# Second attention scores: each head alone on 64 rows of the array instead of both heads on 128 rows

## The chip, the core and the metric

The kernel runs on one core of a Trainium2 chip. A core has a matrix engine (TensorE; PE for its matmuls and PEld for its weight loads in the profile), VectorE (DVE), ScalarE (ACT), GpSimd (POOL) and a queue engine (SP) that issues most DMAs. Matmuls write to PSUM, which has eight banks of 128 partitions by 512 fp32 values; VectorE and ScalarE read the banks out. The metric is device time in microseconds of the one core, and less is better.

## The reference

Two attentions follow each other, and then two mixer layers. With 8 batches, 8 heads, 576 positions, head size 64 and 32 packing vectors per head:

```python
def sm_attn(qq, kk, vv):
    s = scale * np.matmul(qq, kk.transpose(0, 1, 3, 2))
    s = s - np.max(s, axis=-1, keepdims=True)
    a = np.exp(s)
    a = a / (np.sum(a, axis=-1, keepdims=True) + 1e-09)
    return np.matmul(a, vv)
p_packed = sm_attn(p, k, v)                # 32 rows per head over 576 keys
out = sm_attn(q, p_packed, p_packed)       # 576 rows per head over those 32
...
x = mixer_1(x)   # r * v: sigmoid(xr @ w_r) * (relu(xk @ w_k)**2 @ w_v), xk and xr mixed with the row before
x = mixer_2(x)   # u + relu(u @ w_ch1) @ w_ch2, with u = x + its low-rank mix over positions
```

The scores of the second attention, `qq @ kk.T` with 576 queries, 32 keys and 64 terms per head, are what the change is about. They are computed in plain fp32.

## The kernel before, in words

**Units.** A unit of attention is two batches (`b2`) by two heads (`h`). There are 16 units. The generator `attention_steps` writes one: it transposes keys, packing vectors and queries on the matrix engine, makes the first scores in `sps` (two banks), their softmax, the packed rows `pp` (128 x 128: 64 rows a batch, 32 a head; a mask `hmask` zeroes, in each row, the 64 columns of the other head), their transpose `ppt`, and then the second scores. `qt` holds the transposed queries: rows 0 to 63 are head 0, rows 64 to 127 head 1. The softmax of the second scores is `a2` (20 groups of 32 keys, in the order column block, batch, head), which is transposed into `th` and multiplied with `ppz` to give `xo`.

**The stretch of the change.** Line 197 records every matmul, line 209 every transpose. Before, eight matmuls multiply a 128 x 128 block of `qt` with 64 columns of `ppt` (both heads of a batch) into the bank `psa`, and one more with 128 columns into `psb`. The zeroes in `ppt` keep the heads apart. Then VectorE takes, bank by bank, the maximum of each group of 32 (line 274, `s2`) and subtracts it (line 251, into `a2`). In fp32 a matmul is two records of PE and two of PEld in the trace, so the nine are 18.

**Stages.** The first eight units run at the start, four at a time in lanes of their own buffers, advanced by turns: each `yield` of the generator ends a turn. In this stage inputs and weights are loaded and cast, and the first mixer's `psr` matmuls come in between. The other eight units run in the middle of the first mixer's matmuls (`psk`, `psv`, `psr`, `psu`), with two banks for themselves (`ps_a`). After them comes the second mixer (`psc`).

**What sets the order.** Everything is recorded in a plan first. `emit` then walks through a model of the engines: each operation has a cost, an engine takes the ready operation of the lowest class and, on the matrix engine and the SP queue, the lowest sequence number, and a bank is granted to the request that can have it earliest. The engines then execute the written order. So a change of an operation's cost or of the number of turns moves other work as well, most of all in the first stage.

Of the kernel before, what the change touches and what calls it, by code (L numbers as in the profile page):

```python
# [14 lines left out]
ALU = mybir.AluOpType  # L15
# [459 lines left out]
def packed_attention_moe_mixer_kernel(  # L475
# [19 lines left out]
    NP = p.shape[2]  # L495
    P = 128
# [20 lines left out]
    plan = Plan(nc)  # L517
    add, sub, mul = ALU.add, ALU.subtract, ALU.mult
# [35 lines left out]
    def ps_att():  # L554
        return plan.bank(att_banks[0], "psat", att_banks[0] is ps_a)
# [89 lines left out]
    def attention_steps(A, u, u_next):  # L645
# [7 lines left out]
        qt, at = A.big(F32, "qt"), A.big(F32, "at")  # L653
# [37 lines left out]
        for b2 in range(2):  # L691
            for h in range(2):
                o = slice(b2 * 64 + h * 32, b2 * 64 + (h + 1) * 32)
                for r in range(2):
# [3 lines left out]
                            start=True, stop=True, skip_group_check=True)  # L698
        for b2 in range(2):
            for h in range(2):  # L700
                o = slice(b2 * 64 + h * 32, b2 * 64 + (h + 1) * 32)
# [12 lines left out]
        for b2 in range(2):  # L714
            r = slice(b2 * 64, (b2 + 1) * 64)
# [32 lines left out]
        for t in range(5):  # L748
            for g in range(4):
                o = t * P + g * 32  # L750
# [3 lines left out]
                        start=(t == 0), stop=(t == 4), skip_group_check=True)  # L754
# [11 lines left out]
        ppt = plan.tile(A.one, [P, P], F32, "ppt")  # L766
        plan.copy(ppt, ps[:, 0:P])

        yield
        psa = ps_att()  # L770
        for ip in range(4):
            for b2 in range(2):
                plan.mm(psa[:, ip * P + b2 * 64:ip * P + (b2 + 1) * 64],
                        qt[:, b2 * 512 + ip * P:b2 * 512 + (ip + 1) * P],
                        ppt[:, b2 * 64:(b2 + 1) * 64], start=True, stop=True)
        yield
        psb = ps_att()
        plan.mm(psb[:, 0:P], qt[:, 1024:1152], ppt, start=True, stop=True)
        if A.first:
            a2 = A.big(F32, "a2", (0, 1))[:, 0:20 * NP].rearrange("p (g k) -> p g k", k=NP)  # L780
        else:
            a2 = plan.tile(A.one, [P, 20, NP], F32, "a2", parts=(0, 1))
        s2 = plan.tile(A.one, [P, 4, 20], F32, "s2", parts=(0, 1))
        for g, src, g0, g1 in ((0, psa, 0, 16), (1, psb[:, 0:P], 16, 20)):
            sv = src.rearrange("p (g k) -> p g k", k=NP)
            plan.reduce(s2.at(g)[:, 0, g0:g1], sv, ALU.max)
            plan.tt(a2.on(g)[:, g0:g1, :], sv,
                    s2.at(g)[:, 0, g0:g1].unsqueeze(2).to_broadcast([P, g1 - g0, NP]), sub)
        plan.act(a2, a2, AF.Exp, scale=SCALE)
        plan.reduce(s2[:, 1, :], a2, add)  # L790
        plan.ts(s2[:, 2, :], s2[:, 1, :], 1e-9, None, add)
# [14 lines left out]
        for b2 in range(2):  # L806
            r = slice(b2 * 64, (b2 + 1) * 64)
# [7 lines left out]
        for c0, c1 in ((256, 576), (0, 256)):  # L815
# [4 lines left out]
            for n, (lh, rh) in enumerate(terms):  # L820
                for b2 in range(2):
                    r = slice(b2 * 64, (b2 + 1) * 64)
                    plan.mm(pss[b2][:, 0:w], ppz[r, lh, :], rh[r, c0:c1], start=(n == 0),
                            stop=(n + 1 == len(terms)))
# [7 lines left out]
    def attention(A, u, u_next):  # L832
        for _ in attention_steps(A, u, u_next):
            pass
# [104 lines left out]
    plan.cls = 0  # L939
    A0.after = go  # L940
    steps = [attention_steps(lane[u], u, nxt[u]) for u in range(NLEAD)]
    prev = {w: u for u, w in nxt.items()}
    step = 0
# [47 lines left out]
    for b2 in range(2):  # L991
        r = slice(b2 * 64, (b2 + 1) * 64)
# [5 lines left out]
    for i0, i1 in ((0, NI),):  # L998
        src = uv[:, i0 * NP:i1 * NP]
# [360 lines left out]
    for n in range(2, len(chunks)):  # L1360
# [32 lines left out]
        if n >= CAST0:  # L1393
            plan.cls = 3
            for _ in range(len(casts) if n == NCAST else NPER):
                if casts:
                    rows, src, size, put = casts.pop(0)
# [119 lines left out]
```

## Time and profile before

| what | value |
|---|---|
| median of 3 runs | 1522.26 us (1520.06 to 1522.84) |
| the profiled execution | 1520.6 us, of which its span 1518.8 us |
| matrix engine, matmuls | 1486.8 us busy, 98% of the span |
| VectorE | 926.4 us busy, 61% |
| ScalarE | 692.2 us busy, 46% |
| granted clock of the matrix engine | 0.985 of full speed on average |

A busy share says how long an engine had something to do, not that it worked at its peak. A group row reads: line, engine, operation, output<-inputs, shapes, count, then busy time and mean duration in ns, then the idle time just before these instructions and what ended it. In a row of a matmul, `128*128` is the number of rows and columns of the array that it uses, and what follows is the shape that it streams.

### The profile page before, as it was taken

The page shows a single profiled execution, that of the slowest core. Times are in us where ns is not written, and L with a number is a line of the kernel's source. Part 1 is how long each engine was busy: PE and PEld are TensorE (multiplying, and loading weights), DVE is VectorE, ACT ScalarE, POOL GpSimd, SP SyncE. Part 2 cuts the span into 40 slices and gives each one's busy share as a digit, 9 for nine tenths or more (in the row PEclk, how much of TensorE's full clock was granted, in tenths as well). Part 3 has the DMA queues.
Part 4 walks back from the last instruction along what each step waited for, and adds up shares of the span by engine and source line. Part 5 has one row for each costly group of instructions (what it writes and reads, how often), then busy time and mean ns, then how long its engine had stood idle before and what let it go on. Part 6 is the DMA issues. An engine that isn't in the chain of part 4 may idle for free.

```text
span 1518.8 us, 25744 instructions
## 1 busy us (share of the span) xinstructions
PE 1486.8 (98%) x9456; PEld 1300.8 (86%) x9456; DVE 926.4 (61%) x2092; ACT 692.2 (46%) x1595; POOL 269.3 (18%) x522
## 2 busy tenths in 40 slices
PE   6899999999999999999999999999999999999998
PEld 5668888888888888889899898989999999989997
DVE  6687967778777878776645363545435454444533
ACT  5577556666676666666422232322223232322321
POOL 0000000000000000001333333333333333333331
PEclk8689999999999999999999999999999999999999
DMA  9973354664754446666969677696867768676763
GB/s 226 233 184 131 106 134 115 185 177 125 202 154 135 157 130 207 212 217 193 313 160 243 160 199 196 167 242 159 232 159 212 184 169 222 164 216 163 203 168 103
DMA packets 202188, 275.66 MB, mean 181 GB/s; under 512 B 68944, under 2 KB 95888, under 8 KB 202064
## 3 DMA queue, kind: packets, MB, share of 16 engines
q0 software_dynamic: 72576, 132.15, 33.9%
q1 hardware_dynamic: 129488, 141.87, 31.8%
q8 instruction: 76, 1.25, 0.3%
q14 instruction: 48, 0.39, 0.1%
HBM read 221.45 MB, written 52.50 MB: 180 GB/s over the span
## 4 chain that ended last, share of the span: by engine, by line
PE 92%; DMA 3%; DVE 2%; SPq 1%; ACT 1%; issue 1%; DVEq 0%
PE psc L197 49%; PE psk L197 13%; PE psv L197 13%; PE psr L197 6%; PE psat L197 5%; PE psat L209 3%; DMA qin<-in_q_dram 1%; PE psh L197 1%; PE pst L209 1%; SPq L316 1%; PE psu L197 1%; DMA kin<-in_k_dram 1%; DMA s<-w_d 1%; DMA st<-in_moe_w_r_dram 0%; DMA raw_v<-v_d 0%
## 5 line engine op out<-in xcount | busy, mean ns | idle before, releaser
L197 PE MATMUL psc<-w,hid 128*128 128x512 f32 x1728 | 446.6, 393 | 0.7 <-ACT xu L285 0.7
L197 PEld LDWEIGHTS psc<-ob,wb 128*128 128x128 f32 x3024 | 406.7, 190 | 27.1
L197 PE MATMUL psc<-ob,wb 128*128 128x256 f32 x3024 | 420.3, 283 | 0.0
L316 POOL DMA_DIRECT2D wb<-ws_d x504 | 266.2, 529 | 585.1 <-PE psc L197 491.1
L197 PEld LDWEIGHTS psc<-w,hid 128*128 128x128 f32 x1728 | 306.0, 189 | 51.6 <-ACT xu L285 1.1
L197 PE MATMUL psk<-xk,wk 128*128 128x384 f32 x1056 | 210.3, 341 | 2.0 <-DVE wk L270 1.6
L251 DVE TENSOR_TENSOR tmp<-tmp,psc 128x256 f32<-128x256 f32 x288 | 120.8, 420 | 143.5 <-PE psc L197 140.9
L197 PE MATMUL psv<-wv,kk 128*128 128x512 f32 x783 | 205.9, 398 | 0.0
L230 ACT ACTIVATE hid<-tmp 128x256 fp32r<-128x256 f32 x216 | 85.2, 417 | 262.8 <-DVE tmp L251 262.6
L197 PEld LDWEIGHTS psk<-xk,wk 128*128 128x128 f32 x1056 | 184.2, 188 | 11.1 <-DVE wk L270 2.2
L197 PEld LDWEIGHTS psv<-wv,kk 128*128 128x128 f32 x783 | 143.5, 188 | 29.1 <-issue 1.4
L270 DVE SCALAR_TENSOR_TENSOR hid<-psc,hid 128x256 fp32r<-128x256 f32 x72 | 30.5, 424 | 187.6 <-ACT hid L230 187.6
L197 PE MATMUL psr<-wr,xr 128*128 128x512 f32 x414 | 110.9, 401 | 1.4 <-ACT rs L285 0.6
L285 ACT ACTIVATE tmp<-psc 128x256 f32<-128x256 f32 x144 | 54.6, 379 | 125.2 <-PE psc L197 125.2
L270 DVE SCALAR_TENSOR_TENSOR hid<-tmp,hid 128x256 fp32r<-128x256 f32 x216 | 86.4, 423 | 23.3 <-ACT hid L230 15.0
L308 POOL MEMSET x<- 128x8 f32 x4 | 0.5, 114 | 550.6 <-DVE m L267 375.8
L197 PEld LDWEIGHTS psr<-wr,xr 128*128 128x128 f32 x414 | 75.1, 188 | 19.1 <-ACT rs L285 1.2
L230 ACT ACTIVATE sq<-psk 128x384 f32<-128x384 f32 x96 | 46.6, 490 | 68.8 <-PE psk L197 68.1
L230 ACT ACTIVATE hid<-psc 128x256 fp32r<-128x256 f32 x72 | 27.5, 382 | 102.1 <-PE psc L197 102.0
L251 DVE TENSOR_TENSOR kk<-sq,kk 128x384 fp32r<-128x384 f32 x87 | 47.9, 553 | 35.9 <-ACT kk L285 35.8
L267 DVE SCALAR_TENSOR_TENSOR m<-x,mu_t,m 128x384 f32<-128x384 f32 x88 | 52.1, 611 | 0.9 <-ACT m L230 0.7
L230 ACT ACTIVATE m<-x,om_t 128x384 f32<-128x384 f32 x88 | 50.6, 607 | 1.5 <-DVE xr L251 0.9
(174 smaller groups left out, 1704.4 us busy)
## 6 DMA issues: line engine op xcount, KB each, us to landing
wb<-ws_d POOLq DMA_DIRECT2D x504, 256.0 KB, 3.1
st<-in_moe_w_ch_dram SPq DMA_DIRECT2D x32, 512.0 KB, 5.2
ws_d<-wb SPq DMA_DIRECT2D x56, 256.0 KB, 3.0
qin<-in_q_dram SPq DMA_DIRECT2D x32, 288.0 KB, 6.4
x_d<-xo SPq DMA_DIRECT2D x16, 576.0 KB, 3.8
x_d<-x SPq DMA_DIRECT2D x36, 256.0 KB, 2.2
u<-x_d SPq DMA_DIRECT2D x36, 256.0 KB, 5.9
out_dram<-u SPq DMA_DIRECT2D x36, 256.0 KB, 3.8
```

What stands on the lines that cost most here:

```text
L197: self.nc.tensor.matmul(o, l, r, start=start, stop=stop, **k)
L209: self.nc.tensor.transpose(out.get(), in_.get(), ident.get())
L230: self.nc.scalar.activation(o, in_.get(), func, **k)
L251: return self.elem(engs, lambda e, o, x, y: e.tensor_tensor(out=o, in0=x, in1=y, op=op), out, [a, b], self.TT, cls)
L267: ("dve",), lambda e, o, x, y, z: e.scalar_tensor_tensor(out=o, in0=x, scalar=z, in1=y, op0=op0, op1=op1), out, [a, b, s], {"dve": (1.042, ...
L270: ("dve",), lambda e, o, x, y: e.scalar_tensor_tensor(out=o, in0=x, scalar=s, in1=y, op0=op0, op1=op1), out, [a, b], self.TT, cls)
L285: self.nc.scalar.activation(o, i, AF.Copy)
L308: (self.nc.gpsimd if eng == "pool" else self.nc.vector).memset(o, 0.0)
L316: (self.nc.sync if eng == "sp" else self.nc.gpsimd).dma_start(out=o, in_=i)
```

## The change

Each head gets a bank of its own, `ph[0]` and `ph[1]`. Each matmul now uses the 64 rows of one head of `qt` and the 32 keys of that head of one batch, so the nine matmuls become 20. Heads alternate in the written order. Both banks are asked for at once, and one `yield` goes. VectorE again does two maxima and two subtractions, now of 320 values each, and the subtraction writes every second group of `a2`.

```diff
         yield
-        psa = ps_att()
+        ph = [ps_att() for _ in range(2)]
         for ip in range(4):
             for b2 in range(2):
-                plan.mm(psa[:, ip * P + b2 * 64:ip * P + (b2 + 1) * 64],
-                        qt[:, b2 * 512 + ip * P:b2 * 512 + (ip + 1) * P],
-                        ppt[:, b2 * 64:(b2 + 1) * 64], start=True, stop=True)
-        yield
-        psb = ps_att()
-        plan.mm(psb[:, 0:P], qt[:, 1024:1152], ppt, start=True, stop=True)
+                for h in range(2):
+                    r = slice(h * 64, (h + 1) * 64)
+                    o = b2 * 64 + h * 32
+                    plan.mm(ph[h][:, ip * 64 + b2 * 32:ip * 64 + (b2 + 1) * 32],
+                            qt[r, b2 * 512 + ip * P:b2 * 512 + (ip + 1) * P],
+                            ppt[r, o:o + 32], start=True, stop=True, skip_group_check=True)
+        for b2 in range(2):
+            for h in range(2):
+                r = slice(h * 64, (h + 1) * 64)
+                o = b2 * 64 + h * 32
+                plan.mm(ph[h][:, 256 + b2 * 32:256 + (b2 + 1) * 32], qt[r, 1024:1152],
+                        ppt[r, o:o + 32], start=True, stop=True, skip_group_check=True)
...
-        for g, src, g0, g1 in ((0, psa, 0, 16), (1, psb[:, 0:P], 16, 20)):
-            sv = src.rearrange("p (g k) -> p g k", k=NP)
-            plan.reduce(s2.at(g)[:, 0, g0:g1], sv, ALU.max)
-            plan.tt(a2.on(g)[:, g0:g1, :], sv,
-                    s2.at(g)[:, 0, g0:g1].unsqueeze(2).to_broadcast([P, g1 - g0, NP]), sub)
+        av = a2.rearrange("p (g h) k -> p g h k", h=2)
+        for h in range(2):
+            sv = ph[h][:, 0:320].rearrange("p (g k) -> p g k", k=NP)
+            mx = s2.at(h)[:, 0, h * 10:(h + 1) * 10]
+            plan.reduce(mx, sv, ALU.max)
+            plan.tt(av.on(h)[:, :, h, :], sv, mx.unsqueeze(2).to_broadcast([P, 10, NP]), sub)
```

In the order of the matrix engine, this is the ninth unit, in the middle of the first mixer, before. A row is line, operation, output<-inputs, the partitions and columns of the output, and the count; `psv` and `psk` are the mixer's matmuls and `psat` is any bank of attention:

```order
L209 MATMUL psat<-ident,pp 128x128
L197 MATMUL psv<-wv_1894,kk 128x512 x6
L197 MATMUL psk<-xk,wk_1_1890 128x384
L197 MATMUL psat<-ppt,qt 128x64 x8
L197 MATMUL psat<-ppt,qt 128x128
L197 MATMUL psk<-xk,wk_1_1890 128x384 x2
```

And the same place of the changed kernel:

```order
L209 MATMUL psat<-ident,pp 128x128
L197 MATMUL psv<-wv_1968,kk 128x512 x6
L197 MATMUL psat<-ppt,qt 128x32 x20
L197 MATMUL psk<-xk,wk_1_1964 128x384 x3
```

The nine matmuls became 20 in one piece, between the same neighbours give or take one `psk`; all eight units of this stage look like this.

In the first stage the order moves more. The matrix engine about the seventh unit, before (`psr` belongs to the mixer, `a_178` and `a_1385` are the first and the second softmax of two units, `th,ppz` is the last product of a unit):

```order
L197 MATMUL psat<-th,ppz 128x256 x2
L197 MATMUL psr<-wr_184,xr 128x512 x2
L209 MATMUL psat<-ident,pp 128x128
L197 MATMUL psr<-wr_181,xr 128x512 x3
L197 MATMUL psr<-wr_182,xr 128x512
L197 MATMUL psat<-ppt,qt 128x64 x5
L209 MATMUL psat<-ident,a_178 128x128 x2
L209 MATMUL psat<-ident,a_1385 128x128 x4
L209 MATMUL psat<-ident,a_178 128x128 x2
L209 MATMUL psat<-ident,a_1385 128x128
L197 MATMUL psat<-ppt,qt 128x64 x3
```

And the changed kernel about the same unit:

```order
L209 MATMUL psat<-ident,pp 128x128
L197 MATMUL psr<-wr_184,xr 128x512 x4
L197 MATMUL psat<-ppt,qt 128x32 x2
L197 MATMUL psat<-th,ppz 128x320 x2
L197 MATMUL psat<-ppt,qt 128x32 x14
L197 MATMUL psat<-th,ppz 128x256
L197 MATMUL psat<-ppt,qt 128x32 x2
L197 MATMUL psat<-th,ppz 128x256
L197 MATMUL psat<-ppt,qt 128x32 x2
L197 MATMUL psr<-wr_181,xr 128x512 x3
```

The second scores of one unit are cut into four pieces there, with the last products of another unit between them (which also use 64 rows), and the transposes that stood between them before stand elsewhere.

## Rows read from the trace of the kernel before

**Rows 1.** The page: busy time, share of the span and instructions of each engine.
```profile
PE 1486.8 (98%) x9456; PEld 1300.8 (86%) x9456; DVE 926.4 (61%) x2092; ACT 692.2 (46%) x1595; POOL 269.3 (18%) x522
```
**Rows 2.** The page: the chain that ended last, shares of the span.
```profile
PE 92%; DMA 3%; DVE 2%; SPq 1%; ACT 1%; issue 1%; DVEq 0%
```
**Rows 3.** Busy time by stage: from:to and length, engines in turn, clock, DMA share, GB/s.
```profile
0.00:60.00 60.00, 43.06 (x451) 33.88 (x451) 39.28 (x109) 36.34 (x106) 1.31 (x11) 0.85 0.96 221
60.00:86.00 26.00, 21.68 (x94) 15.07 (x94) 15.05 (x35) 12.12 (x35) 0.00 (x0) 0.50 1.11 264
86.00:140.00 54.00, 51.73 (x515) 39.40 (x514) 47.14 (x117) 42.75 (x114) 0.00 (x0) 1.00 0.49 141
230.00:545.00 315.00, 314.25 (x2117) 265.05 (x2116) 243.18 (x544) 207.56 (x462) 0.12 (x1) 1.00 0.53 153
22.00:28.00 6.00, 5.76 (x26) 4.98 (x26) 4.20 (x11) 3.07 (x9) 0.00 (x0) 0.50 1.09 242
```
**Rows 4.** Waits of PE in 0 to 150 us, the longest: total, times, longest.
```profile
PE psat L209 <- DMA kin<-in_k_dram: 7.7, 3, 3.7
PE psat L209 <- DMA qin<-in_q_dram: 5.1, 4, 1.6
```
**Rows 5.** Waits of PE in 230 to 545 us, all of them.
```profile
PE psu L197 <- DVE xs L288: 0.5, 1, 0.5
PE psu L197 <- DVE xs L251: 0.2, 1, 0.2
```
**Rows 6.** Timeline of PE at a late unit: start, length, engine, what, count.
```profile
520.46 2.17 PE L197 MATMUL psat<-ppt,qt 128*128 128x64 f32 x18
522.38 0.71 PE L197 MATMUL psv<-wv,kk 128*128 128x512 f32 x2
```
**Rows 7.** The same for PEld, with the mixer's loads after it.
```profile
520.24 2.20 PEld L197 LDWEIGHTS psat<-ppt,qt 128*128 128x128 f32 x18
522.36 0.30 PEld L197 LDWEIGHTS psv<-wv,kk 128*128 128x128 f32 x2
522.70 2.17 PEld L197 LDWEIGHTS psk<-xk,wk 128*128 128x128 f32 x12
524.86 1.98 PEld L197 LDWEIGHTS psv<-wv,kk 128*128 128x128 f32 x9
```
**Rows 8.** Timeline of PE at an early unit, at half clock.
```profile
62.31 4.05 PE L197 MATMUL psat<-ppt,qt 128*128 128x64 f32 x18
66.15 0.85 PE L209 MATMUL psat<-ident,qin 128*128 128x128 f32 x3
```
**Rows 9.** Timeline of PEld at 498.2 us: loads on 64 rows.
```profile
498.21 0.18 PEld L197 LDWEIGHTS psat<-th,ppz 64*128 64x128 f32 x1 [0.37 <-PE psr L197]
498.21 0.29 PEld L197 LDWEIGHTS psat<-tl,ppz 64*128 64x128 f32 x2
498.32 0.33 PEld L197 LDWEIGHTS psat<-th,ppz 64*128 64x128 f32 x2
```
**Rows 10.** Timeline of PE from 505 to 509 us: first scores inside the mixer.
```profile
504.74 1.72 PE L197 MATMUL psk<-xk,wk 128*128 128x384 f32 x9
506.40 0.66 PE L197 MATMUL psat<-kh,pT 64*32 64x256 f32 x16
506.85 0.31 PE L197 MATMUL psat<-kt,pT 64*32 64x64 f32 x8
507.09 1.68 PE L197 MATMUL psk<-xk,wk 128*128 128x384 f32 x8
508.61 0.63 PE L197 MATMUL psu<-xs,ust 128*128 128x512 f32 x2
```
**Rows 11.** The same for PEld.
```profile
506.39 0.18 PEld L197 LDWEIGHTS psat<-kh,pT 64*32 64x32 f32 x16 [0.25 <-issue]
```
**Rows 12.** Groups of VectorE by form, whole span.
```profile
L274 DVE TENSOR_REDUCE s<-psat 128x16 f32<-128x512 f32 x16 | 11.0, 688 | 8.9 <-PE psat L197 8.9
L251 DVE TENSOR_TENSOR a<-psat,s 128x512 f32<-128x512 f32 x16 | 10.9, 683 | 0.0
L274 DVE TENSOR_REDUCE st<-psat 128x1 f32<-128x320 f32 x16 | 7.8, 487 | 7.3 <-PE psat L197 7.1
L274 DVE TENSOR_REDUCE s<-psat 128x4 f32<-128x128 f32 x16 | 4.5, 282 | 0.0
L251 DVE TENSOR_TENSOR a<-psat,s 128x128 f32<-128x128 f32 x16 | 4.5, 282 | 0.0
```

## Prediction

> **What bounds the kernel now.** I read the busy shares first: the matrix engine is busy 98% of the span, VectorE 61% [rows 1]. The chain of waits agrees, with 92% on the matrix engine [rows 2]. But a share is an average over stages, and the second scores run in two of them, so the table by stage comes next [rows 3]. In 230 to 545 us, where the last eight units lie among the mixer's matmuls, the engine is busy 314.25 of 315 us at full clock, and its waits add up to 0.7 us [rows 5]. There every microsecond of matrix work, more or less, is one of the total, and a later result of VectorE costs nothing while other matmuls are at hand. In the first stage it is otherwise. From 0 to 60 us the engine is busy 43 of 60 us and its longest waits are for inputs, 7.7 and 5.1 us [rows 3, 4]; from 60 to 86 us it has half the clock (1.2 of 2.4 GHz) and DMA queues are full; from 86 to 140 us it is busy 51.7 of 54 us at full clock.
>
> **Part 1: the loads of a burst.** Before, a unit's second scores take from 520.46 to 522.38 us, 1.92 us for 18 records, that is 0.107 us each, and the loads come at the same pace: 18 from 520.24, the next group at 522.36 [rows 6, 7]. So the weight loads (128 columns each) set the pace and the matmuls hide behind them: to stream 64 columns takes less time than to load 128. The change makes 20 matmuls, 40 records with 40 loads, of which two at a time lie on different halves of the array. What does a load on 64 rows cost? At 498.21 us two of them, one on each half, start within 0.01 us, and the next pair follows at 498.32 [rows 9]. So the halves do load side by side, and a pair needs about 0.11 us, as one load on 128 rows does: a load on half the rows is not shorter, since it still has 128 columns. Twenty pairs are 20 x 0.11 = 2.2 us. The streaming gets shorter (32 columns in place of 64), but it was hidden already.
>
> The Trainium skill weighs both ways here. "TensorEngine Tiling (Array Packing)", section "Theoretical Speedup", gives up to 2x for row tiling when the contraction is 64 or less, which would make the burst an estimated 0.96 us. Against it, "TensorE: Matmul & The Clock Gate", section "LDWEIGHTS (loading the stationary operand)", says that a load's time goes by its columns, whatever its rows, and the trace agrees with its 0.11 us for a pair on 64 rows. The tiling page's "Instruction Overhead" warns in the same sense not to take a tiling factor from a dimension that is small already.
>
> **Part 2: going into the half-array mode and back.** Before, the burst stands among matmuls on 128 x 128, without a break. After, it needs another division of the array, in which loads don't run ahead. What that costs is seen at the first scores, which are on 64 x 32 [rows 10, 11]: the load engine stands idle for 0.25 us before them. In all: nine psk matmuls from 504.74 at 0.18 us each (12 loads take 2.16 us [rows 7]) end at 506.36; after the burst, eight until 508.61 have their first slot at 508.61 - 1.44 = 507.17. Of these 0.81 us the streaming takes 0.45 (506.40 to 506.85) and about 0.11 for the short ones (two rounds of 64 columns, estimated by the 0.45 for two rounds of 256). About 0.25 to 0.3 us is left for going in and out. I take 0.3, since loads there have 32 columns and here 128.
>
> A burst then costs 2.2 + 0.3 = 2.5 us in place of 1.92: 0.58 more. Eight of them in the mixer, where nothing hides it: +4.6 us. The bounds are as follows. If a pair of loads took half of the 0.11 us, a burst would cost 1.1 + 0.3 = 1.4, that is 0.5 less; if the two halves did not load side by side, 4.4 + 0.3 = 4.7, 2.8 more.
>
> **Part 3: the first stage.** The same work comes with four units up to 86 us and four behind it. Its bursts are cut into pieces, which cost nothing as long as everything is on 128 x 128, but now each piece between other work is a way in and out. Counted in the two orders of the matrix engine, changes of the array's division grow by 17 up to the first psr and by 10 from there to the last of these units; each is half of 0.3. From 86 us on that is 10 x 0.15 + 4 x 0.28 = 2.6 us on an engine that is 96% busy, and I count all of it. Before 86 us it is 17 x 0.15 + 4 x 0.28 = 3.7 us, more for the burst at half clock (3.84 us for 18 records [rows 8], double), of which the waits for inputs hide a part: 17 of the first 60 us and 4 of the next 26 are idle. I take 2 us of it; the ends are 0 and 5.
>
> **Part 4: VectorE, banks, turns.** Removed per unit: 688 + 683 + 282 + 282 = 1935 ns. Added: two maxima and two subtractions of 320 values, 4 x 487 = 1948 ns by the 320-wide maximum [rows 12]. That is no change. The first maximum now waits for nearly the whole burst, where before it waited for the first bank, eight of nine matmuls: some 0.2 us later. In the mixer this is covered by 0.7 us of waits in 315 [rows 5]; without that cover it would be 8 x 0.2 = 1.6 us. Two banks are held in both cases. One yield less moves each later step of a unit one turn ahead; SP's loads change places by a few rows (a qin behind two reads of x), with no bytes more. I take 0 for this, with 3 us to either side, since the idle time that a better order could fill from 86 to 140 us is 54 - 51.7 = 2.3 us.
>
> **Sum.** 4.6 + 2.6 + 2 = +9.2 us. On the profiled execution of 1520.6 us that is 1529.8; the median of the runs is 1.7 us above that execution, so I forecast 1531 us, with 1525 to 1537 as this case's own range.
>
> **The rivals.**
> - *Cheap halves, faster.* A load on 64 rows with short streaming behind it goes at a quicker pace than the trace shows, and a pair costs half, 0.055 us. Then a burst takes 1.4 us, the eight in the mixer give back 4.2, the first stage nothing (its ways in and out eat it): 1518 us. It decides from the point where a pair takes under (1.92 - 0.3) / 20 = 0.08 us. For it: in the trace the 64-row loads stand before matmuls that stream 256 or 320 columns, never 32. Against it: the second pair in [rows 9] came 0.11 us after the first although nothing had to stream yet. The Trainium skill's 2x ("TensorEngine Tiling (Array Packing)", "Theoretical Speedup") would go this way. Chance 13%.
> - *The first stage hides its share.* Inputs bound it and the order fills the gaps: only 4.6 us remain, 1527 us, or 1524 with a lucky order. For it: full DMA queues up to 86 us [rows 3]. Against it: 96% busy from there on. Chance 17%.
> - *The clock falls.* In the early burst at half clock the engine did nothing but second scores for 3.84 us, and the clock stayed low [rows 3, 8]; so this work, even on all rows, did not raise it. On half the rows, the same burst at full clock may let it fall. A stay like 22 to 28 us [rows 3] costs 3 us; at half of the bursts this is 8 x 3 = 24 us more, 1555; once or twice, 1537. Against it: the first scores (64 x 32) and the last products (64 x 128) stand in the mixer at full clock from 230 to 545 us. Chance 12%.
> - *The halves don't run side by side* when the matmuls are short: +2.8 us a burst, 16 of them, 1567 us. [rows 9] speak against it. Chance 4%.
>
> **How the numbers follow.** The forecast has 54%. Within 0.2% of before, about what a measurement of this kernel can tell from no change, is 1519.2 to 1525.3: some of the second rival (its lower part) and the edge of the first and of the forecast, 14%. Faster: most of the first rival and a lucky order, 15%. Slower: 71%. For 8 times in 10 the range goes from 1518, below which most of the cheap halves lie, to 1542, above which are the many falls of the clock and the serial halves.
>
> **What would show it.** PE and PEld each have 16 x 22 = 352 records more. A late burst of 40 records lasts 2.1 to 2.3 us from its first record to its last, with pairs of loads 0.11 us apart and a gap of about 0.25 us ahead of it; 230 to 545 us gets about 4.6 us longer with waits as small as now. The clock in that stage stays at 1.00. The end of the first eight units moves by 3 to 7 us. I am wrong if pairs of loads come at 0.08 us or less, if the clock's row in the mixer is below 1.00, or if the first stage ends no later than now.

## The result and the profile after

The change made the kernel slower: 1538.08 us median (1532.12 to 1543.68, 4 runs) against 1522.55 (1520.06 to 1523.3, 4 runs), a ratio of 1.0116 with a 95% interval of 1.0093 to 1.0138. A second series on another occasion gave 1541.62 us (1539.42 to 1545.81, 4 runs), ratio 1.0141 (1.0124 to 1.0158). The sign is the one forecast. The two medians lie within 1518 to 1542 us, the range for 8 times in 10, but above 1525 to 1537, the case's own range, and the loss is 15.5 and 20.2 us by the medians where +9 was forecast. In the first series the runs also lie 3.6 times as far apart as those of before (11.6 us against 3.2).

The page of the changed kernel, its first line of busy times, beside [rows 1]:

```profile
PE 1501.8 (98%) x9808; PEld 1312.4 (86%) x9808; DVE 927.9 (61%) x2102; ACT 690.4 (45%) x1585; POOL 269.4 (18%) x522
```

The matrix engine has the 352 records more that were counted on, and 15 us more of busy time; VectorE has no more to do.

A late unit of the changed kernel on PE, to be read against [rows 6]:

```profile
529.71 1.12 PE L197 MATMUL psk<-xk,wk 128*128 128x384 f32 x5
530.76 2.42 PE L197 MATMUL psat<-ppt,qt 64*128 64x32 f32 x40
533.11 0.62 PE L197 MATMUL psk<-xk,wk 128*128 128x384 f32 x2
```

And on PEld, against [rows 7]:

```profile
530.76 2.31 PEld L197 LDWEIGHTS psat<-ppt,qt 64*128 64x128 f32 x40 [0.25 <-issue]
533.11 0.48 PEld L197 LDWEIGHTS psk<-xk,wk 128*128 128x128 f32 x3
```

From the first record to the next work it is 2.35 us in place of 1.92, and the load engine stands idle for 0.25 us before. That is the burst of the forecast: 20 pairs of loads, 0.11 us apart, and a way in and out.

The stages of the changed kernel, in the columns of [rows 3]:

```profile
0.00:60.00 60.00, 45.24 (x479) 35.51 (x479) 36.71 (x104) 34.31 (x101) 1.32 (x11) 0.83 0.97 224
60.00:86.00 26.00, 21.45 (x196) 14.22 (x194) 20.83 (x50) 16.48 (x43) 0.00 (x0) 0.80 1.05 248
86.00:140.00 54.00, 52.28 (x521) 41.44 (x521) 40.81 (x104) 33.77 (x92) 0.00 (x0) 0.84 0.49 147
230.00:545.00 315.00, 312.54 (x2285) 261.38 (x2284) 241.13 (x544) 202.11 (x450) 0.12 (x1) 1.00 0.54 154
```

The reader is to look at the clock, the third number from the right. In the mixer it is 1.00, as before. From 60 to 86 us it is higher than before (0.80 against 0.50), but from 86 to 140 us, where the engine is busy 97% of the time, it is 0.84 against 1.00: some 17 of these 54 us at 1.2 GHz. This is the fastest but one of eight runs (1533.45 us). The profile of the second series shows the slowest one (1545.81 us), in the same view:

```profile
0.00:86.00 86.00, 67.27 (x613) 51.67 (x614) 52.92 (x141) 44.97 (x123) 1.31 (x11) 0.71 0.97 226
86.00:140.00 54.00, 52.55 (x522) 40.23 (x521) 36.74 (x96) 32.36 (x95) 0.00 (x0) 0.78 0.48 132
0.00:150.00 150.00, 129.83 (x1192) 99.49 (x1193) 99.19 (x258) 85.09 (x234) 1.31 (x11) 0.75 0.75 185
```

Where a run lost its time can be told by two landmarks, the first `psu` (the mixer is well under way, the first eight units are done) and the first `psc` (the second mixer begins). The engine has the same records between them in both kernels, but for those of the change. In these rows the shortest, median and longest duration in ns come first, then the first and the last start in us. The kernel before:

```profile
L197 PE MATMUL psu<-xs,ust x72: 390/397/505, 219.0 to 735.5; 128*128 128x512 f32 x72
L197 PE MATMUL psc<-ob,wb x3024: 274/283/368, 721.0 to 1510.3; 128*128 128x256 f32 x189
```

The changed kernel, first series:

```profile
L197 PE MATMUL psu<-xs,ust x72: 390/397/504, 225.7 to 748.3; 128*128 128x512 f32 x72
L197 PE MATMUL psc<-ob,wb x3024: 274/283/365, 733.7 to 1523.2; 128*128 128x256 f32 x189
```

The changed kernel, second series:

```profile
L197 PE MATMUL psu<-xs,ust x72: 389/397/506, 235.3 to 757.9; 128*128 128x512 f32 x72
L197 PE MATMUL psc<-ob,wb x3024: 273/283/417, 743.4 to 1535.5; 128*128 128x256 f32 x189
```

Between the landmarks lie 502.0, 508.0 and 508.1 us: the mixer with the late units costs 6 us more, and it costs this in both. Up to the first landmark it is 6.7 us more in the one and 16.3 in the other. So the mixer has a fixed price near the forecast, and most of what was missed, and of what differs from run to run, is in the first stage. Another 2.6 us of the slower run lie behind the second landmark: there the matrix engine waits 2.2 us for `xu` (0.7 in the kernel before), and a stay of 3.4 us at half clock follows.

### The profile page after: what moved, and what is told of

Read it like the earlier page. It is cut to its first block, busy times and chain, and to the rows that moved or that the text cites. A ratio compares the mean times of both kernels' runs of the same rounds, so it can differ in the third digit from the quotient of the medians.

```text
span 1531.7 us, 26453 instructions
## 1 busy us (share of the span) xinstructions
PE 1501.8 (98%) x9808; PEld 1312.4 (86%) x9808; DVE 927.9 (61%) x2102; ACT 690.4 (45%) x1585; POOL 269.4 (18%) x522
## 4 chain that ended last, share of the span: by engine, by line
PE 92%; DMA 3%; DVE 2%; SPq 1%; ACT 1%; issue 1%; DVEq 0%; ACTq 0%
PE psc L197 49%; PE psk L197 13%; PE psv L197 13%; PE psr L197 7%; PE psat L197 5%; PE psat L209 3%; DMA qin<-in_q_dram 1%; PE psh L197 1%; PE pst L209 1%; PE psu L197 1%; SPq L316 1%; DMA s<-w_d 1%; DMA kin<-in_k_dram 0%; DMA vin<-in_v_dram 0%; DMA st<-in_moe_w_v_dram 0%
## 5 line engine op out<-in xcount | busy, mean ns | idle before, releaser
L197 PEld LDWEIGHTS psat<-ppt,qt 64*128 64x128 f32 x640 | 44.2, 196 | 8.1 <-issue 2.2
```

Source lines behind the costliest of these rows:

```text
L197: self.nc.tensor.matmul(o, l, r, start=start, stop=stop, **k)
```

## Experiments

Ratios are to runs of the kernel before in the same series (medians 1520.5 to 1521.4 us). "Clock" is the median over a kernel's runs of the mean granted clock; before it is 0.987 or 0.988. The first row, "streams twice", "four times, first eight units" and "heads in turn" are of one series; the two stages alone, the turns and "four times" of another; the last three rows of two more.

| kernel | median us | ratio (95%) | clock |
|---|---|---|---|
| as changed, again | 1541.62 | 1.0141 (1.0124 to 1.0158) | 0.978 |
| late eight units alone | 1527.91 | 1.0054 (1.0039 to 1.0069) | 0.986 |
| first eight units alone | 1528.36 | 1.0042 (1.0024 to 1.0060) | 0.980 |
| old matmuls, new turns and banks | 1516.40 | 0.9969 (0.9952 to 0.9986) | 0.990 |
| each new matmul streams twice | 1532.95 | 1.0086 (1.0067 to 1.0104) | 0.986 |
| four times | 1530.17 | 1.0071 (1.0059 to 1.0083) | 0.991 |
| four times, first eight units | 1530.76 | 1.0069 (1.0056 to 1.0082) | 0.991 |
| heads in turn | 1575.95 | 1.0365 (1.0334 to 1.0396) | 0.965 |
| order of before, half the streaming | 1521.04 | 1.0006 (0.9995 to 1.0017) | 0.985 |
| changed order, 128 rows | 1522.81 | 1.0013 (1.0002 to 1.0025) | 0.990 |
| changed order, 128 rows, half the streaming | 1526.73 | 1.0030 (1.0017 to 1.0043) | 0.984 |

**The change in one of the two stages.** Both sets of matmuls and of VectorE's operations stand in the code, and the unit decides:

```diff
+        new = u >= NLEAD      # the other kernel: u < NLEAD
+        if new:
             ph = [ps_att() for _ in range(2)]
             ...
+        else:
+            psa = ps_att()
             ...
```

> The change in the last eight units alone (those in the middle of the first mixer); the first eight are as before, in the same order on the matrix engine. Theory (two costs that add: a fixed one of a burst in the mixer, and one of the first stage that came out larger than forecast): each late burst costs 0.4 to 0.55 us more, 8 of them 3.5 to 4.5 us, so about 1526.5 us, with the clock at full speed through the mixer. Rival (the clock falls in the mixer, or later work there is delayed): more than 8 us, 1530 us or above. Rival (the late part is hidden and all of the loss is in the first stage): within 1 us of before.

> The change in the first eight units alone; the matrix engine's order is that of the changed kernel up to the mixer. Theory: it carries the larger part of the loss and its spread, 8 to 15 us, so 1530 to 1538 us, with runs apart by several us, the slower ones at a lower mean clock. Rival (the first stage costs what was forecast, 4.6 us, and the rest comes later): 1527 us with a spread as before, 3 us.

The late units cost 8.2 us by the ratio, the first eight 6.4, together 14.6 of the 18 to 21 by the ratios of the whole change. The late bursts last 2.35 us each and the mixer is at full clock, as the theory has it; between the landmarks there are 506.7 us, 4.7 more than before. The other 3.5 us by the ratio were not expected. The profiled run of it was its slowest (1531.67 us). In it 2.8 us more than before lie behind the second landmark, with a wait of 2.1 us for `xu` as above, and it has two stays at half clock outside the units (0.83 over 10 us, at 170 and at 745 us). How much of this the faster runs have isn't known.

The first eight alone gave runs from 1520.88 to 1532.0 us, at clocks of 0.987 and 0.975; the late eight alone lie from 1523.94 to 1531.67. So the larger part of the spread is the first eight's, but not all. The median of this kernel, 1528.36 us, is under the 1530 of my theory and close to the rival's 1527. Up to the first landmark this kernel does need 10.9 us more than before (229.9 us), as the theory has it; but between the landmarks it needs 498.4 us, 3.6 less than before, with the same matmuls there. What differs there is the written order of the mixer, which the first stage shifts: it is worth some 4 us by itself.

**The turns and banks alone.**

```diff
         yield
-        psa = ps_att()
+        psa, psb = [ps_att() for _ in range(2)]
...
-        yield
-        psb = ps_att()
         plan.mm(psb[:, 0:P], qt[:, 1024:1152], ppt, start=True, stop=True)
```

> The matmuls as before (nine on 128 rows, psa and psb), but both banks asked for at once and one yield less, as in the change. Theory (the new matmuls are the cause): within 3 us of before, 1520 to 1526 us. Rival (the order that one turn less gives is the cause in the first stage): 1528 us or more, with the first stage later by 5 us or more.

It is 0.3% faster than before, 4 us by the medians, 1 beyond my 3. The matmuls are to blame, then, not the turns. Its landmarks:

```profile
L197 PE MATMUL psu<-xs,ust x72: 387/393/501, 219.5 to 732.2; 128*128 128x512 f32 x72
L197 PE MATMUL psc<-ob,wb x3024: 274/283/365, 717.7 to 1506.6; 128*128 128x256 f32 x189
```

The gain is in the mixer (498.2 us, 3.8 less than before). The matrix engine's waits for `xs` are down to 0.2 us from 0.7 there [rows 5], which is 0.5 of it; what makes up the rest no run here shows. This is the version that beats both kernels.

**The clock, by what is streamed.** A burst's pace is set by its loads, so that each matmul can stream its 32 columns again, onto columns of the bank that a later one overwrites (`REP` is 4 or 2; the last four matmuls of a unit get the same edit, which is left out here):

```diff
-                    plan.mm(ph[h][:, ip * 64 + b2 * 32:ip * 64 + (b2 + 1) * 32],
+                    plan.mm(ph[h][:, ip * 64 + b2 * 32:ip * 64 + b2 * 32 + 32 * REP].rearrange("p (a k) -> p a k", k=NP),
                             qt[r, b2 * 512 + ip * P:b2 * 512 + (ip + 1) * P],
-                            ppt[r, o:o + 32], start=True, stop=True, skip_group_check=True)
+                            ppt[r, o:o + 32].unsqueeze(1).to_broadcast([64, REP, NP]),
+                            start=True, stop=True, rep=REP, skip_group_check=True)
...
```

> The changed kernel, same order, same loads, same rows, but each of its matmuls streams its 32 columns four times over (128 columns; the copies fall on columns of the bank that a later matmul overwrites or nobody reads). The loads at 0.11 us a pair should hide this, so a burst takes at most 0.1 to 0.2 us more. Theory (in the first stage the clock is lower where time counts, since bursts on half the rows keep the array little occupied): the stretch behind 86 us is at full clock in more of the runs, and the time falls by 5 to 10 us, to 1526 to 1531 us, with less spread. Rival (the clock goes by something else, such as waits for inputs, or the first stage is longer because of its ways in and out alone): as the changed kernel, 1532 to 1544 us, with the same spread.

> The changed kernel once more, for the spread and the mean clock of each run. Theory (its first stage runs at half clock for a time that differs from run to run): 1531 to 1544 us, the runs in the order of their mean clock (0.988 down to 0.975), with about 5 to 6 us for each 0.005 of it. Rival (the spread has another cause): runs of the same clock differ by 5 us or more.

> As the changed kernel, each new matmul streaming its 32 columns twice (64 columns). Rows times columns streamed in a burst are then those of the kernel before. Theory (the clock goes by what the array streams): the mean clock lies between that of the changed kernel (0.976 to 0.988) and of the one with four times (0.990 to 0.993), and the median between theirs, 1530 to 1536 us. Rival (a threshold between one and two times): as with four times, 1529 to 1531 us. Rival (streaming is not what counts, the earlier gain was chance): as the changed kernel, 1533 to 1542 us.

> Four times the streaming in the first eight units alone. Theory (it is the first stage whose clock counts): as with four times everywhere, or 0.6 us less for the late bursts, 1528 to 1531 us with a mean clock of 0.99. Rival (the mixer's clock counts too): as the changed kernel.

With the same order and the same loads, the array doing more useless work, the kernel gets faster: 1541.62 us (1538.08 in the first series), 1532.95 with twice the streaming, 1530.17 with four times, at clocks of 0.978, 0.986 and 0.991. One of the six runs with twice the streaming, 1540.49 us at 0.978, is still as slow as the changed kernel. Four times in the first eight units alone does the same as four times everywhere, so it is the first stage that matters. Four times, by stage, against the rows of the changed kernel above:

```profile
0.00:86.00 86.00, 64.50 (x665) 47.64 (x665) 57.69 (x153) 50.15 (x141) 1.32 (x11) 0.82 1.01 231
86.00:140.00 54.00, 52.13 (x550) 40.89 (x551) 44.37 (x112) 38.09 (x101) 0.00 (x0) 0.99 0.47 147
```

The stretch from 86 us on is back at 0.99. A closer look shows where the changed kernel lost it. Two stretches of its first profile:

```profile
86.00:97.00 11.00, 11.00 (x116) 9.19 (x115) 7.71 (x21) 6.48 (x20) 0.00 (x0) 1.00 1.06 276
97.00:107.00 10.00, 9.42 (x89) 6.63 (x89) 5.81 (x18) 4.88 (x15) 0.00 (x0) 0.51 0.35 98
```

and the second of them with four times the streaming:

```profile
97.00:107.00 10.00, 9.27 (x135) 6.70 (x134) 7.20 (x23) 5.81 (x18) 0.00 (x0) 1.00 0.34 94
```

Up to 97 us the engine is busy without a break at full clock. The last thing that it does there is second scores:

```profile
91.84 2.42 PE L197 MATMUL psat<-ppt,qt 64*128 64x32 f32 x20
94.19 0.74 PE L197 MATMUL psr<-wr,xr 128*128 128x512 f32 x2
94.86 2.19 PE L197 MATMUL psat<-ppt,qt 64*128 64x32 f32 x18
```

Then the clock falls to half. With four times the streaming the same pieces lie from 93.4 to 98.7 us, and the clock stays at full speed behind them. The price of streaming is small (a late burst of the kernel with four times):

```profile
526.69 2.50 PE L197 MATMUL psat<-ppt,qt 64*128 64x128 f32 x40
529.12 0.62 PE L197 MATMUL psk<-xk,wk 128*128 128x384 f32 x2
```

2.43 us against 2.35. The repeated run of the changed kernel came out in the order of its clocks (0.979 twice, 0.977, 0.975: 1539.42, 1540.40, 1542.84, 1545.81 us). From 0.979 to 0.975 the time rises by 5.4 to 6.4 us, a little more than the 5 to 6 expected for each 0.005. At the other end, 0.988 and 0.984 of the first series, it was 1.3 us for 0.004.

**Do the halves run side by side?** The loops over heads and blocks change places. As the last four matmuls have a loop of their own, the order is eight matmuls on the lower rows, eight on the upper, then two and two (not ten and ten, as the expectation has it):

```diff
-        for ip in range(4):
-            for b2 in range(2):
-                for h in range(2):
+        for h in range(2):
+            for ip in range(4):
+                for b2 in range(2):
...
-        for b2 in range(2):
-            for h in range(2):
+        for h in range(2):
+            for b2 in range(2):
```

> The heads one after the other: ten matmuls on rows 0 to 63, then ten on rows 64 to 127, else as changed. If two loads on different halves run side by side only when their matmuls alternate, a late burst takes 40 x 0.11 = 4.4 us in place of 2.35, and 16 of them cost 20 to 33 us more than the changed kernel: 1555 to 1575 us. Rival (the engine lets loads run ahead far enough that the halves overlap all the same): a burst of 2.4 us, and the time of the changed kernel.

A late burst of this kernel, and the clock in three stretches with such bursts in the mixer:

```profile
257.95 3.78 PE L197 MATMUL psat<-ppt,qt 64*128 64x32 f32 x40
261.66 0.61 PE L197 MATMUL psk<-xk,wk 128*128 128x384 f32 x2
```

```profile
255.00:275.00 20.00, 20.00 (x139) 17.64 (x128) 14.67 (x33) 9.71 (x21) 0.00 (x0) 0.91 0.01 2
305.00:318.00 13.00, 13.00 (x79) 11.45 (x78) 7.97 (x18) 5.09 (x10) 0.00 (x0) 0.87 0.67 188
390.00:400.00 10.00, 10.00 (x64) 9.00 (x63) 6.40 (x15) 4.22 (x10) 0.00 (x0) 0.83 0.67 141
```

3.71 us, between the two cases but nearer to the serial one: the alternation is what lets the halves overlap. In this burst the loads come one by one, 0.11 us apart, except for four pairs where the lower rows give way to the upper (from 259.28 us) and four where they come back (from 260.65): 32 steps for 40 loads. And here the clock falls in the mixer too. At six of the eight late bursts a stay at half clock begins, in the burst or within 1.2 us of its end, while the engine is busy all the time. The median, 1575.95 us, is 1 us above my range, although the burst is shorter than I had it; the clock of 0.965 is the likely reason.

**Streaming or rows?** Two kernels halve the streaming and leave the 128 rows; both leave out second scores of head 1 (the first of them in eight of its nine matmuls). That one has the order of before (the edit of VectorE's reads is left out here):

```diff
-                plan.mm(psa[:, ip * P + b2 * 64:ip * P + (b2 + 1) * 64],
+                plan.mm(psa[:, ip * P + b2 * 64:ip * P + b2 * 64 + 32],
                         qt[:, b2 * 512 + ip * P:b2 * 512 + (ip + 1) * P],
-                        ppt[:, b2 * 64:(b2 + 1) * 64], start=True, stop=True)
+                        ppt[:, b2 * 64:b2 * 64 + 32], start=True, stop=True, rep=2)
...
```

> The kernel before with half the streaming: the eight matmuls of a bank stream only the 32 columns of head 0 (all 128 rows, same loads, same order, no change of the array's division), and VectorE reads these scores for both heads, so head 1's second scores are left out. The engine has no more to do than before: by the loads' pace of 0.11 us a burst lasts as long. Theory (the clock goes by what the array streams): in the first stage it stays at half clock longer, the mean clock falls to 0.975 to 0.985 and the time rises by 5 to 15 us, to 1526 to 1536 us, with no work added. Rival (what lowers the clock is the half rows or the changes of division, not the streaming): as before, 1518 to 1523 us at 0.985 to 0.991.

My theory failed here in the time: 0.06% with an interval across no change. The clock did fall, 0.985 against 0.988 in its series, at the upper edge of what I expected, but in the order of before the first stage takes this almost without loss. So the last two keep the changed kernel's order, row by row, and put ten matmuls on 128 rows in it (one for each pair of places of the order; the other place stays empty):

```diff
+        for n in range(10):
+            ...
+            keys = slice(b2 * 64, b2 * 64 + 64)     # half: + 32
+            for h in range(2):
+                ...
+                    if h == n // 5:
+                        nc.tensor.matmul(to.get(), qt[:, cols].get(), ppt[:, keys].get(), ...)
+                plan.add(("pe",), fn, (qt, ppt), (ph[h],))
```

> The changed kernel's written order, with each pair of its matmuls (the two heads of a batch) replaced by one of the old kind: 128 rows, both heads, 64 columns, no change of the array's division. A burst is ten matmuls, 20 records at 0.107 us, 2.1 us. Theory (the half rows with their ways in and out, not the order around them, lower the clock and add the work): mean clock 0.986 to 0.991, 1518 to 1524 us, that is 15 us or more under the changed kernel. Rival (the order of the changed kernel does it): mean clock 0.975 to 0.982, 1530 us or more.

> The same with 32 columns streamed in place of 64 (head 0's scores are read for both heads, head 1's are left out): what the rows stream in a burst is halved, as in the changed kernel, with all rows, the same loads and no change of division. Theory A (streaming counts in this order, though it hardly did in the order of before): mean clock 0.003 or more under that of the kernel with 64 columns, and 4 us or more slower. Theory B (it is the stops at each change of division that count, and streaming more in the half-row kernel only made up for them): clock and time within 2 us of the kernel with 64 columns.

In the changed order the old matmuls take 1522.81 us at 0.990. So the order, together with bursts of 20 records in place of 18, costs 0.13%, by its interval 0.25% at the most, and the half rows, which stream 32 columns a matmul, carry the rest. Their profile up to 150 us, with 64 and then with 32 columns:

```profile
0.00:150.00 150.00, 127.38 (x1130) 100.28 (x1131) 108.01 (x279) 100.13 (x263) 1.31 (x11) 0.90 0.78 196
```

```profile
0.00:150.00 150.00, 130.03 (x1112) 101.69 (x1113) 107.05 (x276) 96.03 (x255) 1.31 (x11) 0.83 0.75 191
```

Half the streaming lowers the clock from 0.990 to 0.984 (runs from 0.988 to 0.992 against 0.982 to 0.990) and costs 3.9 us by the medians, 2.6 by the ratios. The intervals of the ratios overlap, so of the two the fall of the clock is the better shown. It is theory A in sign, a little under its size in time. It does not bring all of the changed kernel's fall, which goes to 0.978. What is left comes with the half rows: the stops at each change of division, the longer stage, or both; no run here takes these apart.

## Why the prediction was wrong in size, by its own steps

**Part 1 and 2, the burst: right.** 20 pairs at 0.11 us, a gap of 0.25 us, and 2.35 us against 1.92. With the first record 0.1 us later behind the one before it, that is 0.53 us more for each burst, where 0.58 was forecast. The halves do load side by side, and the rival of cheap halves had no part in it.

**The mixer, +4.6 us: nearly right.** 6.0 us between the landmarks. The 8 bursts make 8 x (0.43 + 0.1) = 4.2. The rest is the order's, for which Part 4 had 0 with 3 to either side. The old matmuls in the changed order show it:

```profile
L197 PE MATMUL psu<-xs,ust x72: 390/397/509, 217.0 to 737.1; 128*128 128x512 f32 x72
L197 PE MATMUL psc<-ob,wb x3024: 274/283/384, 722.5 to 1512.5; 128*128 128x256 f32 x189
```

They need 505.5 us between the landmarks, 3.5 more than before. Bursts of 2.15 us in place of 1.92 make 8 x 0.23 = 1.8 of it, and 1.7 is left for the order. A part of it is seen in the waits. From 230 to 545 us they were 0.7 us [rows 5] and became 2.5 in this view of the changed kernel (from 219 to 735 us, over the whole mixer, it is 1.6 and 2.5):

```profile
PE psu L197 <- DVE xs L288: 1.7, 4, 0.5
PE psu L197 <- DVE xs L251: 0.5, 2, 0.2
PE psk L197 <- ACT sq L230: 0.3, 1, 0.3
```

The old matmuls in the same order have the same three rows.

**Part 3, the first stage, +2.6 + 2 us: this step failed.** Its work was priced at the clock that the trace of before had in each stretch, and the sum had no term for a change of that clock. The change took this clock away from the stage. Up to 150 us these are the kernel before and the first series of the changed kernel:

```profile
0.00:150.00 150.00, 126.46 (x1115) 98.06 (x1116) 107.06 (x270) 99.57 (x269) 1.31 (x11) 0.85 0.78 193
0.00:150.00 150.00, 128.96 (x1245) 99.67 (x1246) 104.44 (x269) 91.70 (x249) 1.32 (x11) 0.84 0.76 189
```

The kernel before stood at 0.85 and the changed kernel at 0.75 in its second series (its row is shown above), that is 2 x 150 x 0.10 = 30 us more at half clock, which cost up to 15 us, and the first landmark is 16.3 us later, not 3 to 7. In the first series the total at half clock was nearly that of before (0.84), but 17 us of it had moved into the stretch from 86 us on; that its landmark moved by 6.7 us, inside the 3 to 7 forecast, is luck. With the clock given back (four times the streaming) the change costs 1530.2 to 1530.8 us, within 1 us of the forecast of 1531, but this too is in part luck: that kernel has a better clock than before had (0.991 against 0.987). At a clock like that of before (twice the streaming, 0.986) the median is 1533.0. So, as an estimate, about 2 us are work, ways in and out and order that I had too low, 1.4 of them in the mixer, and the clock is the other 5 to 9 (1533.0 against 1538.1 and 1541.6).

**The rival "the clock falls" had the mechanism and the wrong place.** I read from [rows 3, 8] that second scores on all rows did not raise a low clock, and gave 12% to a fall at the bursts on half the rows, with the mixer's clock as its sign. There it stayed at 1.00. The rival's smaller case, a fall once or twice, was priced at 1537 us, near the 1538 of the first series. The same two rows spoke more loudly of the first stage: there the clock already went up and down before, so a little less streaming had something to change. I had the rows and put the rival where dense matmuls stand on both sides. "The first stage hides its share" was wrong for the same reason: the stage ended later by 6.7 and 16.3 us.

**Part 4, VectorE and turns: right but for the size of the order.** VectorE's share did not change, and the turns alone gave -0.3%, just outside the 3 us, on the side of a gain; in the changed kernel the mixer's order cost 1.7 us.

## What to carry to other kernels

Where loads set the pace, as here, halving rows and columns of a matmul gained nothing: compare the distance of two loads with the time to stream, and count the loads. Before pricing an edit in a stretch whose clock goes up and down in the trace, treat the clock as an outcome of the edit and not as a given: take the sum at both levels, and expect a wider spread of runs. A test for it is cheap where loads set the pace, since the array can stream the same columns again for almost nothing (four times cost 0.08 us a burst here).

## What the runs showed of the hardware that was not expected

- More work on the array made a kernel faster: with four times the columns streamed in the first eight units, 0.7% less time in the same series (1.0069 against 1.0141), at a mean clock of 0.991 against 0.978. Against the first series of the changed kernel (1.0116) it is 0.5%.
- With heads in turn the clock fell at six of eight late bursts of 3.7 us or more, in the midst of dense matmuls (0.83 to 0.91 over the stretches shown), with the engine never idle.
- Where the written order goes from one half of the rows to the other, a few loads of the two halves still ran side by side: four pairs at each of two such places out of three, so that 40 records took 3.71 us and not the 4.4 of 40 loads one after the other.
